# A gated attention unit with a low-rank mixer: the start of the first batch rearranged

## The chip, the cores and the metric

The kernel runs on one core of a Trainium2 chip. The metric is the device time of one execution in microseconds (us). The engines are named as in the profile: PE (TensorE, matrix multiplication), DVE (VectorE), ACT (ScalarE), POOL (GpSimd) and SP (SyncE). POOL and SP here mostly issue transfers; each works through its own queue in order.

## The reference

There are 8 batches, a sequence of S = 3136, a width of 256, and 64 columns in z. Everything comes in and goes out as float32.

```python
scores = (1/S) * z @ z.T                 # per batch, 3136 x 3136, symmetric
attn   = max(scores, 0) ** 2
x      = u * (attn @ v)                  # 3136 x 256
h      = (x.T @ U @ V).T                 # U: 3136 x 32, V: 32 x 3136
y      = x + h
out    = y + max(y @ w_ch1, 0) @ w_ch2   # w_ch1: 256 x 1024, w_ch2: 1024 x 256
```

## The kernel before

**Tiles.** The sequence is cut into 25 tiles: 24 full ones of 128 rows and a last one of 64, whose rows are held twice. All products are in bfloat16. `zT` holds z transposed, with its 64 columns in both halves of the 128 partitions, so that two score matmuls run in the two halves of PE at a time (`score`, L272). ACT applies the ReLU with the scale 1/S (L291) and DVE squares in place (L293). Since the scores are symmetric, only 13 of 25 blocks of each row are computed: `A[j]` is the panel of tile j, with the blocks at distances 0 to 12. The others come by a DMA transpose of a panel into a `strip` (`turn`, L313), issued by SP.

**Attention.** An output tile o is a sum over 25 blocks (`half`, L351), in two halves of PE, into two PSUM banks; two output tiles make a pair. `close_pair` (L365 to L375) adds the two banks (an ACT copy, a DVE add) and multiplies by u on DVE. There are two sets of banks, so a pair can be opened only when the one two before it has been added. Scores are written to PSUM by way of `pair_psum`, which has two buffers.

**Main loop.** For each batch, output tiles are taken in the order 12, 13, ..., 24, 0, ..., 11, while scores of this and the next batch, and the mixer of the batch before, are mixed in between. All five engines' instructions stand in the order in which the program issues them: there is no scheduler, so each engine's order is the order of the calls.

**The start (`start_up`, L607).** In batch 0 no scores exist yet, so the first eight output tiles are made in another way.

1. POOL loads z in three parts, tiles 8 to 16, 0 to 8, 16 to 24, with a cast to bfloat16 (L174), and v in six (L225). DVE copies z twice side by side (`double_z`, L188), PE transposes it against a unit matrix (`turn_on_pe`, L204), and ACT or DVE casts the result into zT (L212).
2. *Side blocks.* For the output tiles 12 to 15, `make(pair)` computes the scores of two tiles j against the four tiles, and `use(pair)`, two pairs later, adds them to the four accumulators. Those of tiles 3 to 11 belong into their panels; the others have room in `v_both[1]` (v of batch 1, not loaded yet) and `x_bf` (L639 to L641). Steps of the list `nxt` stand between: the full score panels of tiles 16 to 19, each with its strip. Then both pairs are closed, one after the other (L686).
3. *Stored blocks.* For the output tiles 16 to 19, `use_stored` takes blocks that lie in panels, `make_stored` computes more of them two pairs ahead, and the remaining twelve blocks of each come from strips (`tail`).
4. Between 2 and 3, w2 is loaded, and z of batch 1 is doubled and transposed as a whole (L695, L696).

The loads of v of batch 1 are issued from the main loop of batch 0 (`v_at`, L781), one part at a time.

Of the kernel before, what the change touches and what calls it, by code (L numbers as in the profile page):

```python
# [42 lines left out]
def kernel(  # L43
# [11 lines left out]
    nc = tc.nc  # L55
# [113 lines left out]
    def load_z(b, parts):  # L169
        if b not in z_raw:  # L170
            z_raw[b] = stage.tile([P, NT, dqk], BF16, name="z_c")
        z_c = z_raw[b]
        for t0, t1 in parts:
            pool_dma(out=z_c[:, t0:t1, :], in_=rows(z[b])[:, t0:t1, :])  # L174
            if t1 == NF:
                for r in halves:
                    pool_dma(out=z_c[r, NF, :], in_=z[b, NF * P :, :])
# [14 lines left out]
    def turn_z(b, parts):  # L192
        z_bf = z_tiles[b]
        for t0, t1 in parts:
            transpose(
                out=zT_of(b)[:, t0 : upto(t1), :],
                in_=z_bf[:, t0 : upto(t1), :, :].rearrange("p t h c -> p (t h c)"),
            )
    def turn_on_pe(parts, banks):

        z_bf = z_tiles[0]
        for (t0, t1), ps in zip(parts, banks):
            for t in range(t0, t1):
                mm(  # L204
                    out=ps[:, (t - t0) * P : (t - t0 + 1) * P],
                    lhsT=z_bf[:, t, :, :].rearrange("p h c -> p (h c)"),
                    rhs=eye,
                    start=True,
                    stop=True,
                )  # L210
            copy = nc.vector.tensor_copy if t0 % 8 else nc.scalar.copy
            copy(  # L212
                out=zT_first[:, t0:t1, :].rearrange("p t c -> p (t c)"),
                in_=ps[:, : (t1 - t0) * P],
            )
# [390 lines left out]

    def start_up():  # L607
        parts = ((8, 16), (0, 8), (16, NF))
        load_z(0, parts[:2])
        nc.gpsimd.memset(eye, 1.0)  # L610
        nc.gpsimd.affine_select(
            out=eye,
            in_=eye,
            pattern=[[1, P]],
            base=0,
            channel_multiplier=-1,
            compare_op=ALU.is_equal,
            fill=0.0,
        )
        load_v(0, (8, 12))  # L620
        load_v(0, (12, 18))
        load_z(0, parts[2:])
        for part in [(3, 8), (0, 3), (18, NF), (NF, NT)]:
            load_v(0, part)
        double_z(0, parts[:2])
        turn_on_pe([(8, 12), (12, 16)], sets[0])
        turn_on_pe([(0, 4), (4, 8)], sets[1])
        nc.gpsimd.memset(U_bf[:, NF, :], 0.0)
        outs = [FIRST + i for i in range(NG)]
        c0 = FIRST * P  # L630
        for o in outs[::2]:
            open_pair(0, o)
            load_u(0, o)
        if B > 1:
            load_z(1, WHOLE)
        for s in fetches[:3]:
            s()
        nxt = [s for j in range(LEAD, LEAD + NG) for s in turned(0, j)]
        rooms = [v_both[1][:, t : t + 4, :] for t in range(0, NF, 4)]  # L639
        rooms = [r.rearrange("p (a t) d -> p a (t d)", a=2) for r in rooms]  # L640
        rooms += [x_bf[:, g].rearrange("p (a w) -> p a w", a=2) for g in (2, 3)]  # L641
        pairs = [(8, 9), (10, 11), (12, 13), (14, 15), (6, 7), (3, 4), (5,), (1, 2)]
        pairs += [(0, 16), (17, 18), (19, 20), (21, 22), (23, 24)]
        where = {}

        def make(pair):
            if all(LEAD - 1 - HALF <= j < FIRST for j in pair):
                todo = []
                for j in pair:
                    at = (FIRST - j) * P  # L650
                    where[j] = A[j][:, at : at + NG * P]
                    todo.append((j, c0, NG * P, where[j]))
                score(0, todo)
            else:
                room = rooms.pop(0)
                for i, j in enumerate(pair):
                    where[j] = room[:, i, :]
                score(0, [(j, c0, NG * P, room) for j in pair])

        seen = []  # L660

        def use(pair):
            for j in pair:
                for o in outs:
                    at = (o - FIRST) * P
                    stop = [o % 2 == 1 and len(seen) == NT - 1 - h for h in range(2)]
                    beside(o, j, where[j][:, at : at + P], stop)
                seen.append(j)

        for i, pair in enumerate(pairs):  # L670
            if i == 3:
                double_z(0, parts[2:])
            if i == 5:
                ps = pair_psum()
                turn_on_pe([(16, 20), (20, NF)], [ps[:, 0, :], ps[:, 1, :]])
                turn_on_pe([(NF, NT)], [pair_psum()[:, 0, :]])
                extend_z(0)
            make(pair)
            if i > 5 and i % 2:
                nxt.pop(0)()  # L680
            if i > 1:
                use(pairs[i - 2])
        for pair in pairs[-2:]:
            nxt.pop(0)()
            use(pair)
        for o in outs[1::2]:  # L686
            close_pair(0, o)

        outs = [LEAD + i for i in range(NG)]
        for o in outs[::2]:  # L690
            open_pair(0, o)
            load_u(0, o)
        fetches[3]()
        if B > 1:
            double_z(1, WHOLE)  # L695
            turn_z(1, WHOLE)  # L696
        pairs = [(j, j - 1) for j in range(LEAD - 1, LEAD - FIRST, -2)]

        def use_stored(js):
            for j in js:  # L700
                for o in outs:
                    if 0 <= o - j <= HALF:
                        beside(o, j, block(0, o, j))

        def make_stored(pair):
            todo = []
            for j in pair:
                k0, k1 = LEAD - j, min(NB, LEAD + NG - j)
                todo.append((j, LEAD * P, (k1 - k0) * P, A[j][:, k0 * P : k1 * P]))
            score(0, todo)  # L710

        nxt += [lambda pair=pair: make_stored(pair) for pair in pairs[:2]]
        own = [lambda j=j: use_stored([j]) for j in outs]
        for s in _merge(nxt, own):
            s()
        rest = []
        for j in range(FIRST - NG, LEAD):
            rest += score_steps(0, j, LEAD + NG - j, NB)
        more = [s for j in range(LEAD + NG, LEAD + 2 * NG) for s in score_steps(0, j)]
        for i, pair in enumerate(pairs):  # L720
            if i + 2 < len(pairs):
                make_stored(pairs[i + 2])
            else:
                more.pop(0)()
            use_stored(pair)
            if i == len(pairs) - 1:
                turn(0, LEAD + NG)
        tail = []
        for o in outs:
            js = [(o + 1 + i) % NT for i in range(HALF)]  # L730

            def close(o=o, j=js[-1]):
                beside(o, j, block(0, o, j), [o % 2 == 1] * 2)
                if o % 2:
                    close_pair(0, o)
                if o == outs[1]:
                    load_u(0, LEAD + NG)
                if o < outs[-1]:
                    turn(0, o + NG + 1)

            for i in range(3):
                some = js[4 * i : min(4 * i + 4, HALF - 1)]
                tail.append(lambda o=o, js=some: [beside(o, j, block(0, o, j)) for j in js])
            tail.append(close)
        for s in _merge(tail, more + rest):
            s()
# [20 lines left out]
    def run(steps):  # L767
        for s in steps:
            s()
# [5 lines left out]
    for b in range(B):  # L775
# [2 lines left out]
        bursts = bursts_of(b - 1) if b else []  # L778
        burst_at = {4: (0, 1), 8: (2, 3), 13: (4, 5), 17: (6, 7)}
        own = own_at if b else first_at  # L780
        v_at = dict(zip((9, 11, 12, 14, 16, 18, 20, 22, 23), V_PARTS)) if b == 0 else {}  # L781
        ahead = dict(zip((2, 3, 6, 7, 10, 11, 14), range(NC)))
        for i in range(begin, NT):
            o = turns(i)
            fill = [s for key in own.get(i, ()) for s in score_steps(b, *key)]
            if more:
                fill += [s for key in next_at[i] for s in score_steps(b + 1, *key)]
                if b and i == 1:
                    load_z(b + 1, WHOLE)
                if b and i == 7:  # L790
                    turn_z(b + 1, ((FIRST, NF),))
                if b and i == 10:
                    turn_z(b + 1, ((0, FIRST),))
                if i == 11:
                    extend_z(b + 1)
                if i in v_at:
                    load_v(b + 1, v_at[i])
            main = attend_steps(b, o)
            if b and i in ahead:
                main.insert(17 if (i + (i > FIRST)) % 2 == 0 else 10, lambda c=ahead[i]: low_rank(b - 1, c))  # L800
# [74 lines left out]
```

## Time and profile before

| | |
|---|---|
| median of 4 runs | 1022.61 us |
| lowest and highest run | 1014.69, 1031.09 us |
| profiled execution | 1012.96 us |
| its span | 1011.3 us |
| PE busy | 986.9 us, 98% of the span |
| ACT busy | 613.3 us, 61% |
| DVE busy | 541.1 us, 54% |
| POOL busy | 171.8 us, 17% |
| moved by DMA | 167.70 MB, mean 166 GB/s |

The profile is that of one execution; its times are counted from the start of its span. A busy share is the time in which an instruction was in work, so a busy engine need not be at its peak. In a line of the order of time the columns are start, duration, engine, line of the program, operation, output and inputs, count, and in brackets the idle time before it with what ended it. Several equal instructions in a row are put together, with their joint duration. A line of a group ends instead with the busy time, the mean of one in nanoseconds, and idle time with what ended most of it. "SPq" is a DMA that SP's queue issued.

### The profile page before, as it was taken

To read this page: it belongs to the slowest core of one execution; us is meant where nothing else is said; L and a number is where in the kernel's file an instruction comes from. 1 tells how busy PE (TensorE), PEld (TensorE's weight loads), DVE (VectorE), ACT (ScalarE), POOL (GpSimd) and SP (SyncE) were. 2 spreads that over 40 slices of the span, in tenths; PEclk is the share of its full clock that TensorE was granted. 3 is DMA by queue.
4 is the path that set the end of the run, shared out by engine and by line. 5 is a ranking of instruction groups with operands and counts; after the bars stand their busy time and mean duration, and the time that the engine had idled before them with its cause. 6 is when DMAs were issued, how large, how long until landed. Compare 5 with 4: busy or idle time off the path is not lost.

```text
span 1011.3 us, 31291 instructions
## 1 busy us (share of the span) xinstructions
PE 986.9 (98%) x13816; PEld 784.8 (78%) x13856; DVE 541.1 (54%) x977; ACT 613.3 (61%) x834; POOL 171.8 (17%) x318
## 2 busy tenths in 40 slices
PE   7799999999999999999999999999999999999998
PEld 5588877787778877788787887878877788777856
DVE  5877654456544664446644556445664356542242
ACT  7886764666645776456764667556674666643154
POOL 4122112121121211121112211112112120011000
PEclk9999999999999999999999999999999999999999
DMA  9999989999998998989989998989989997777532
GB/s 171 153 204 216 185 151 186 179 174 146 165 206 162 176 169 170 166 181 169 160 177 167 182 167 148 191 172 188 151 159 194 168 187 140 143 143 167 105 97 97
DMA packets 414584, 167.70 MB, mean 166 GB/s; under 512 B 389408, under 2 KB 399328, under 8 KB 414448
## 3 DMA queue, kind: packets, MB, share of 16 engines
q1 hardware_dynamic: 384944, 99.16, 61.1%
q0 software_dynamic: 29504, 66.55, 28.5%
q8 instruction: 108, 1.77, 0.7%
q14 instruction: 28, 0.23, 0.1%
HBM read 61.88 MB, written 25.69 MB: 87 GB/s over the span
## 4 chain that ended last, share of the span: by engine, by line
PE 89%; DVE 4%; DMA 3%; ACT 2%; issue 1%; POOL 0%; DVEq 0%; ACTq 0%; POOLq 0%
PE ps L351 46%; PE ps L562 17%; PE ps L520 16%; PE ps L278 6%; ACT A L291 2%; DMA strip<-A 1%; PE ps L385 1%; DVE A L293 1%; PE ps L442 1%; DVE x_bf L502 1%; PE ps L488 1%; DMA out_dram<-o_sb 1%; DVE both L366 1%; DMA zT<-z_bf 1%; DVE x_bf L375 0%
## 5 line engine op out<-in xcount | busy, mean ns | idle before, releaser
L291 ACT ACTIVATE A<-ps 128x832 bf16<-128x832 f32 (+8 forms) x469 | 352.3, 763 | 155.1 <-PE ps L278 141.6
L351 PE MATMUL ps<-v,A 64*128 64x256 bf16 x4864 | 333.1, 269 | 5.8 <-DVE A L293 2.8
L293 DVE TENSOR_TENSOR A<-A 128x832 bf16<-128x832 bf16 (+8 forms) x469 | 240.4, 524 | 146.1 <-ACT A L291 142.1
L351 PE MATMUL ps<-v,strip 64*128 64x256 bf16 x4420 | 306.9, 269 | 0.7 <-DMA strip<-A 0.7
L351 PEld LDWEIGHTS <-A 64*128 64x128 bf16 x4864 | 239.2, 94 | 48.4 <-issue 14.2
L538 ACT ACTIVATE relu_bf<-ps 128x1024 bf16<-128x1024 f32 (+2 forms) x208 | 187.9, 909 | 141.9 <-PE ps L520 139.9
L351 PEld LDWEIGHTS <-strip 64*128 64x128 bf16 x4420 | 222.1, 94 | 34.0 <-DMA strip<-A 0.9
L562 PE MATMUL ps<-w_bf,relu_bf 128*128 128x256 bf16 x1600 | 204.8, 273 | 0.2 <-ACT relu_bf L536 0.2
L573 DVE TENSOR_TENSOR o_sb<-ps,x_bf 128x512 f32<-128x512 f32 (+1 forms) x104 | 69.7, 670 | 248.8 <-PE ps L562 233.7
L520 PE MATMUL ps<-ut,w_bf 128*128 128x512 bf16 (+2 forms) x856 | 197.3, 351 | 2.4 <-ACT relu_bf L538 0.3
L562 PEld LDWEIGHTS <-relu_bf 128*128 128x128 bf16 x1600 | 155.9, 98 | 47.3 <-issue 3.2
L335 POOL DMA_DIRECT2D u_sb<-in_u_dram x96 | 53.4, 556 | 469.3 <-DVE x_bf L375 436.4
L520 PEld LDWEIGHTS <-w_bf 128*128 128x128 bf16 x896 | 85.0, 98 | 61.1 <-issue 7.0
L278 PE MATMUL ps<-zT 64*128 64x416 bf16 (+8 forms) x812 | 131.0, 312 | 0.7 <-ACT A L291 0.7
L365 ACT COPY both<-ps 128x512 f32<-128x512 f32 (+1 forms) x104 | 58.8, 567 | 74.2 <-PE ps L351 66.5
L581 POOL DMA_DIRECT2D out_dram<-o_sb x84 | 46.0, 548 | 272.6 <-DVE o_sb L573 268.6
L366 DVE TENSOR_TENSOR both<-ps,both 128x512 f32<-128x512 f32 (+1 forms) x104 | 69.3, 666 | 27.1 <-ACT both L365 26.7
L375 DVE TENSOR_TENSOR x_bf<-both,u_sb 128x512 bf16<-128x512 f32 (+1 forms) x104 | 69.8, 671 | 3.6
L502 DVE TENSOR_TENSOR x_bf<-ps,x_bf 128x512 bf16<-128x512 f32 (+1 forms) x112 | 65.5, 626 | 8.6 <-PE ps L488 8.6
L278 PEld LDWEIGHTS <-zT 64*128 64x128 bf16 x812 | 42.6, 94 | 4.7 <-issue 0.9
L225 POOL DMA_DIRECT2D v<-in_v_dram x61 | 34.3, 564 | 0.2 <-PE ps L520 0.2
L278 PE MATMUL ps<-relu_bf 64*128 64x416 bf16 (+9 forms) x121 | 22.0, 339 | 2.4 <-ACT A L291 1.3
(52 smaller groups left out, 229.9 us busy)
## 6 DMA issues: line engine op xcount, KB each, us to landing
u_sb<-in_u_dram POOLq DMA_DIRECT2D x96, 256.0 KB, 3.9
out_dram<-o_sb POOLq DMA_DIRECT2D x84, 256.0 KB, 3.2
v<-in_v_dram POOLq DMA_DIRECT2D x57, 192.0 KB, 4.4
strip<-A SPq DMA_TRANSPOSE x196, 5.4
out_dram<-o_sb SPq DMA_DIRECT2D x12, 256.0 KB, 2.1
z_c<-in_z_dram POOLq DMA_DIRECT2D x7, 384.0 KB, 6.1
w_bf<-in_moe_w_ch_dram POOLq DMA_DIRECT2D x2, 512.0 KB, 7.5
u_sb<-in_u_dram POOLq DMA_DIRECT2D x16, 64.0 KB, 2.5
```

What stands on the lines that cost most here:

```text
L278: mm(out=ps[:, k, :n], lhsT=zT[halves[k], j, :], rhs=zT_flat[halves[k], c : c + n], start=True, stop=True,)
L291: nc.scalar.activation(out=dst, in_=src, func=AF.Relu, scale=sc)
L293: nc.vector.tensor_tensor(out=dst, in0=dst, in1=dst, op=ALU.mult)
L351: mm(out=acc[t0][h][:, (o - t0) * D : (o - t0 + 1) * D], lhsT=w[halves[h]], rhs=v_both[b % 2][halves[h], j, :], start=start, stop=stop, **kw,)
L365: nc.scalar.copy(out=both[:, :w], in_=banks[1][:, :w])
L366: nc.vector.tensor_tensor(out=both[:, :w], in0=banks[0][:, :w], in1=both[:, :w], op=ALU.add)
L375: nc.vector.tensor_tensor(out=x_at(b, t0, n), in0=split(both[:, :w]), in1=u_sb[:, :n, :].rearrange("p t (a c) -> p t a c", c=P), op=ALU.mult,)
L502: nc.vector.tensor_tensor(out=q, in0=split(ps[h][:, : len(ks) * D]), in1=q, op=ALU.add)
L520: mm(out=ps[i][:, :w] if apart else ps[:, i, :w], lhsT=w1_bf[:, db, (hp + i) * P : (hp + i + 1) * P], rhs=uT[c][:, db, len(chunks[c]) * P ...
L538: nc.scalar.activation(out=relus[c][:, hp : hp + 2, :w], in_=ps[:, :, :w], func=AF.Relu)
L562: mm(out=ps[:, k * D : (k + 1) * D], lhsT=relus[c][:, ht, q : q + P], rhs=w2_bf[:, ht, :], start=(ht == 0), stop=(ht == NH - 1),)
L573: nc.vector.tensor_tensor(out=o_sb[:p, :nk, :].rearrange("p t (a c) -> p t a c", c=P), in0=split(ps[:p, : nk * D]), in1=x_at(b, t, nk)[:p] ...
```

## The change

All of it lies in `start_up` and its helpers, and in one line of the main loop.

- Tiles 0 to 16 of z of batch 0 are no longer loaded by POOL with a cast, but by SP as float32 into the two buffers for u, and DVE and ACT each make one of the two copies (`first_z`). Ahead of that DVE zeroes 512 columns of a buffer, and PE runs seven matmuls of 512 columns on them whose result is not used.
- Tiles 16 to 24 of z are transposed into one pair of banks and cast by one DVE instruction, not in two groups by ACT and DVE.
- All weights, w2 among them, and then all of v of batch 1, are issued by POOL right after z of batch 1. The loads in the main loop are gone.
- The side blocks that lay in `v_both[1]` and `x_bf` lie in the panels of tiles 20 to 24 and 0 to 2, not yet in use then.
- The last two pairs of side blocks are used first for the output tiles 12 and 13, which are closed, and then for 14 and 15. The stored blocks of step 3 are likewise taken first for 16 and 17. Two steps of `nxt` go ahead of them.
- z of batch 1 is doubled and transposed in two parts, after the second and the third pair of stored blocks.

```diff
+    def first_z(parts):
+
+        z_bf = z_tiles[0] = stage.tile([P, NT, 2, dqk], BF16, name="z_bf")
+        wide = zT_rest[:, :4, :].rearrange("p t c -> p (t c)")
+        nc.vector.memset(wide, 0.0)
+        ps = pair_psum()
+        for _ in range(7):
+            mm(out=ps[:, 0, :], lhsT=zT_rest[:, 0, :], rhs=wide, start=True, stop=True)
+        landed = []
+        for t0, t1 in parts:
+            z_f = u_pool.tile([P, 2, D], FP32, name="u_sb").rearrange("p a c -> p (a c)")
+            z_f = z_f.rearrange("p (t c) -> p t c", c=dqk)
+            nc.sync.dma_start(out=z_f, in_=rows(z[0])[:, t0:t1, :])
+            landed.append(z_f)
+        for (t0, t1), z_f in zip(parts, landed):
+            nc.vector.tensor_copy(out=z_bf[:, t0:t1, 0, :], in_=z_f)
+            nc.scalar.copy(out=z_bf[:, t0:t1, 1, :], in_=z_f)
+
...
-            copy = nc.vector.tensor_copy if t0 % 8 else nc.scalar.copy
+            copy = nc.vector.tensor_copy if t0 % 8 or t1 == NF else nc.scalar.copy
...
-        load_z(0, parts[:2])
+        first_z(parts[:2])
...
-        double_z(0, parts[:2])
         turn_on_pe([(8, 12), (12, 16)], sets[0])
         turn_on_pe([(0, 4), (4, 8)], sets[1])
...
-        for s in fetches[:3]:
-            s()
+        run(fetches)
+        if B > 1:
+            for part in V_PARTS:
+                load_v(1, part)
         nxt = [s for j in range(LEAD, LEAD + NG) for s in turned(0, j)]
-        rooms = [v_both[1][:, t : t + 4, :] for t in range(0, NF, 4)]
-        rooms = [r.rearrange("p (a t) d -> p a (t d)", a=2) for r in rooms]
-        rooms += [x_bf[:, g].rearrange("p (a w) -> p a w", a=2) for g in (2, 3)]
+        rooms = [A[j % NT][:, : 2 * NG * P] for j in range(LEAD + NG, LEAD + 3 * NG)]
+        rooms = [r.rearrange("p (a w) -> p a w", a=2) for r in rooms]
...
             if i == 5:
-                ps = pair_psum()
-                turn_on_pe([(16, 20), (20, NF)], [ps[:, 0, :], ps[:, 1, :]])
+                turn_on_pe([(16, NF)], [pair_psum().rearrange("p a w -> p (a w)")])
...
-        for pair in pairs[-2:]:
+
+        for o in outs[1::2]:
             nxt.pop(0)()
-            use(pair)
-        for o in outs[1::2]:
+            for pair in pairs[-2:]:
+                use(pair, (o - 1, o))
             close_pair(0, o)
...
-        fetches[3]()
-        if B > 1:
-            double_z(1, WHOLE)
-            turn_z(1, WHOLE)
...
-        own = [lambda j=j: use_stored([j]) for j in outs]
-        for s in _merge(nxt, own):
-            s()
+        run(nxt[:2])
+        own = [
+            lambda j=j, some=some: use_stored([j], some)
+            for some in (outs[:2], outs[2:])
+            for j in outs
+            if j <= some[-1]
+        ]
+        run(_merge(nxt[2:], own))
...
-            use_stored(pair)
+            use_stored(pair, outs)
+            if B > 1 and i in (1, 2):
+                part = ((0, FIRST), (FIRST, NF))[i - 1]
+                double_z(1, (part,))
+                turn_z(1, (part,))
...
-        v_at = dict(zip((9, 11, 12, 14, 16, 18, 20, 22, 23), V_PARTS)) if b == 0 else {}
...
-                if i in v_at:
-                    load_v(b + 1, v_at[i])
```

More of the change, by code (lines that the diff above doesn't have):

```diff
@@ L658, in make, with use @@
                 score(0, [(j, c0, NG * P, room) for j in pair])
-        seen = []
-        def use(pair):
+        def use(pair, some):
             for j in pair:
-                for o in outs:
+                for o in some:
                     at = (o - FIRST) * P
-                    stop = [o % 2 == 1 and len(seen) == NT - 1 - h for h in range(2)]
+                    stop = [o % 2 == 1 and j == NF - h for h in range(2)]
                     beside(o, j, where[j][:, at : at + P], stop)
-                seen.append(j)
         for i, pair in enumerate(pairs):
@@ L681, in start_up @@
             if i > 1:
-                use(pairs[i - 2])
-        for pair in pairs[-2:]:
+                use(pairs[i - 2], outs)
+        for o in outs[1::2]:
             nxt.pop(0)()
-            use(pair)
-        for o in outs[1::2]:
+            for pair in pairs[-2:]:
+                use(pair, (o - 1, o))
             close_pair(0, o)
@@ L692, in start_up, with use_stored @@
             load_u(0, o)
-        fetches[3]()
-        if B > 1:
-            double_z(1, WHOLE)
-            turn_z(1, WHOLE)
         pairs = [(j, j - 1) for j in range(LEAD - 1, LEAD - FIRST, -2)]
-        def use_stored(js):
+        def use_stored(js, some):
             for j in js:
-                for o in outs:
+                for o in some:
                     if 0 <= o - j <= HALF:
```

## The prediction

> **What bounds the kernel now.** The engine table of the page comes first: TensorE (PE) is busy for 986.9 us of a span of 1011.3, so all its idle time together is 24.4 us. The table of stretches then shows where that lies (columns: stretch, length, busy time of PE, PE weight loads, DVE, ACT, POOL, clock, DMA share, GB/s).
>
> ```profile
> 0.00:5.00 5.00, 0.00 (x0) 0.00 (x0) 0.56 (x2) 1.28 (x1) 3.83 (x12) 1.00 0.45 55
> 5.00:10.00 5.00, 4.20 (x42) 3.04 (x44) 3.54 (x8) 3.65 (x7) 2.90 (x6) 1.00 1.02 170
> 10.00:15.00 5.00, 3.92 (x60) 2.94 (x58) 3.89 (x9) 3.69 (x7) 3.36 (x7) 1.00 1.12 216
> 15.00:20.00 5.00, 4.40 (x67) 3.50 (x64) 3.11 (x6) 4.50 (x7) 2.30 (x4) 1.00 1.11 241
> 20.00:26.00 6.00, 5.94 (x99) 4.97 (x94) 4.58 (x8) 5.82 (x8) 0.00 (x0) 1.00 0.83 155
> 26.00:34.00 8.00, 4.07 (x50) 2.40 (x47) 7.46 (x14) 5.67 (x10) 2.03 (x3) 1.00 0.63 127
> 34.00:39.00 5.00, 5.00 (x91) 4.48 (x89) 3.65 (x11) 4.57 (x11) 0.00 (x0) 1.00 1.29 144
> 39.00:45.00 6.00, 4.90 (x69) 3.41 (x65) 4.48 (x9) 5.92 (x9) 0.00 (x0) 1.00 1.32 201
> ```
>
> The reader is to see three holes: 5.0 us before the first matmul, 3.9 us of 8 in 26 to 34, where DVE is full (7.46 of 8), and 1.1 us in 39 to 45, where ACT is full. From 60 us on PE has no hole but 0.71 us in 80 to 90, and batches 1 to 6 lose 0.4 to 1.4 us each (120.67 busy of 122, 122.58 of 123). So the change works on the first 60 us, with 13.8 us of idle PE, 5 of them before data. The order of time names what ends each hole:
>
> ```profile
> 5.05 1.89 PE L204 MATMUL ps<-eye,z_bf 128*128 128x128 bf16 x16 [5.05 <-DVE z_bf L188]
> ...
> 29.70 1.87 DVE L188 COPY z_bf<-z_c 128x1600 bf16<-128x1600 bf16 x2
> ...
> 31.60 8.22 SPq L195 DMA_TRANSPOSE zT<-z_bf  x1
> ...
> 32.63 0.28 PE L351 MATMUL ps<-v,A 64*128 64x256 bf16 x2 [1.60 <-DVE A L293]
> ...
> 44.73 0.61 PE L351 MATMUL ps<-v,strip 64*128 64x256 bf16 x8 [0.71 <-DMA strip<-A]
> ```
>
> The first hole waits for z; the second for DVE, which doubles batch 1's z between the closing of two pairs and the next score blocks; the third for a strip transpose queued behind the 8.22 us transpose of batch 1's z.
>
> **Opening.** Before, POOL issues z at 1.30, the chain gives it 3.11 us to 4.41, the doubling ends at 5.05. After, SP issues z in float32 from about 0.8 (its queue waits 0.7 at the start). The nearest row, SP's output stores of 256 KB, has 2.1 us to landing: first part 2.9, second about 4.1 (256 KB more at some 200 GB/s). An ACT copy of 512 float32 takes 0.59 (row of L212), and DVE works beside it: ready at 3.5 and 4.7. The Trainium skill ("Trainium Kernel Development and Optimization", Key Constraints) speaks against a gain here: queues of different engines share the same DMA engines, so another issuer saves only issue time. By that the first part would need POOL's 3.1 us and be ready at 4.5, by the row at 3.5. It hardly matters, since the fill of seven 512-column matmuls takes seven times about 0.43 us (two pairs of such scores took 1.04 us with one latency), 1.1 to 4.1. So PE turns z at 4.1 to 4.5 instead of 5.05.
>
> What the fill itself is worth: the clock column reads 1.00 everywhere, but the same score matmul is longer at first (windows 4.9 to 8.55 and 8.6 to 12.2):
>
> ```profile
> L278 PE MATMUL ps<-relu_bf 64*128 64x512 bf16 x4 | 1.0, 618 | 0.0
> ```
> ```profile
> L278 PE MATMUL ps<-relu_bf 64*128 64x512 bf16 x6 | 1.2, 377 | 0.7 <-ACT A L291 0.7
> ```
>
> The Trainium skill ("TensorE: Matmul & The Clock Gate", Part 1) says that PE runs at half rate until it has been busy for a window of about 3.4 us, free-running, so that its end moves by half a microsecond. By the granted clock the fill gains nothing; by the rule, with which the 618 against 377 ns agree, it takes 0.24 us off the first score and 0.05 us off each transpose. I take the rule. Then: block 8 to 12 turned by 4.6, cast by ACT after its second z copy, 4.7 to 5.3; DVE's cast to 5.6; first score 5.65 instead of 6.87; first ReLU about 6.1 instead of 7.52: 1.4 us. The next release must hold too: v tiles 8 to 12 landed at 7.87 (a POOL wait) for a use at 8.87, tiles 12 to 18 at 10.27 for 11.29. Two z issues of POOL (1.22 us) leave its queue ahead of them, so they should land about 1 us earlier, against uses 1.4 earlier: it holds by about 0.6. I book **-1.3**, between -0.6 (z or v late) and -2.0.
>
> **Turning z tiles 16 to 24 in one piece.** It removes a PE wait of 0.67 between two groups of transposes, and an ACT cast of 0.59; the DVE cast doubles, from 0.69 to at most 1.4. DVE is free for it at 13.2, so it ends near 14.5, where a score took the bank at 14.13 before. **+0.2**, from 0 to +0.4. The eight rooms in panels hold what the v and x buffers held, by the same 1.05 us ReLU and 0.69 us square: no row separates them, 0. No ReLU or square is added or removed.
>
> **Closing interleaved, doubling moved.** From 26.5 DVE has: one square 0.59, four pair operations of 0.685, three squares of 0.59, two of 0.43, together 6.0 us, and 1.87 of doubling. Without it the squares that PE waits for end at 32.5 instead of 33.4. The interleaving lets scores 1.1 us of ACT earlier through, but DVE stays the bound, so only the 0.9 counts. The doubling returns after the second and third stored pair: there PE needs 16 times 0.055 plus 0.21, 1.1 us a pair, 6.5 for six; DVE 4.3 for the squares plus 1.87, 6.2. It fits with 0.3 to spare, and queued behind each copy are the squares two pairs ahead. **-0.8**, from 0 (all given back) to -1.9.
>
> **Order of SP's queue.** Strips 18 and 19 now go ahead of batch 1's transpose, so the 0.71 us stall at 44.73 goes. Next late is strip 20: both z halves (8.22 together) go from about 35.5 to 44, then the strip takes 2.4 (ten in 24.29 us) to 5.4; it is used at 51.75 less the shift, about 49. It fits by 0 to 3 us. **-0.7**, from 0 to -1.1.
>
> **Loads brought forward.** On POOL w2 moves from 30.62 to 18 (0.92 us), and ten issues of v of batch 1 (9 parts, 0.55 us each, 5.4 us in all) from 53 to 97 to behind it. They queue ahead of u for the pairs 16 and 18, issued at 28.75 and 30.09. POOL waits for earlier landings, so bytes set its pace: weights and v, 3.0 MB at about 200 GB/s, 15.4 to 31. u issued at up to 31 lands 4.7 later, and DVE wants it at 45.82: 10 us of cover, cost 0; without cover each microsecond is lost one for one. Strips 16 and 17 share the DMA engines with this burst, and are used at 38.74, 11 us after their time: 0. Later, 1.6 MB of some 9 MB leave 53 to 97, where ACT waits 4.9 us for strips but PE loses only the 0.71: **-0.4**, from 0 to -0.7.
>
> **Sum.** -1.3 +0.2 -0.8 -0.7 -0.4 = -3.0 us. The profiled execution took 1012.96 us (1.66 around the span): 1009.96 after. The four runs have a median of 1022.61, 9.65 above it, and scatter from 1014.69 to 1031.09. I carry the difference over: **1019.6 us**.
>
> **Rivals.** *The opening's holes close as a whole.* Idle PE from 5 to 60 us is 8.8, with 1.3 before and 0.7 in 80 to 90: 10.8, giving 1011.8. For it: every hole named has its cause touched. Against: ACT at 5.82 of 6 and 5.92 of 6, and DVE at 7.46 of 8, fill them with work that is only moved. A variant with the same time: the 9.65 us by which ordinary runs exceed the profiled one are late transfers, and early loads remove most of it; no row shows those runs. Together 0.25.
>
> *SP's queue falls behind, slower.* Place: the line from strip 16 (21.75) to strip 20 (needed at 49), with four strips and z ahead. At the strip median of 2.35 us it holds five strips and z, 20 us of 27; PE waits from a mean of 3.8. With the burst beside it, at 5.4 a strip and z doubled to 16.4, it holds 43.4, 16 late, less 2.3 gained elsewhere: 1036. It is over 1% slower from a mean strip of about 6.4. Against: strips ran at 2.43 with the DMA share at 1.2 to 1.3, and the burst should be over before z turns. With the scatter of the runs, 0.10.
>
> *The change does not do what it says:* z still lands at about 4.4, v binds at 8.87, DVE gives back the doubling: 1022, 0.05.
>
> **How the numbers follow.** The forecast has 0.60. Its parts end at -5.7 and about +0.4, so 1017 to 1023; the scatter of a median of such runs, about 4 us, makes it 1013 to 1027. One percent, 10 us, is about what a measurement of this kernel tells from no change, and it is also nearly all idle time within the change's reach. Reaching toward the first rival, the range is 1009 to 1026. Faster by over 1% 0.25, within 0.65, slower 0.10.
>
> **What would show it.** Right: first transposes of z near 4.1 to 4.5; first score of 512 below 0.45 us; first ReLU near 6.1; use of the first stored pair near 31; no PE wait for a strip below 50 us; no v load between 45 and 100. Wrong: a first wait for v near 7.5, a PE wait for squares behind the doubling, a wait for strip 20, or main-loop idle that differs from 0.4 to 1.4 us a batch.

## The result, and the profile after

The changed kernel is slower by 0.43%: a median of 1020.78 us against 1016.83 us, a ratio of 1.0043 with a 95% interval of 1.0029 to 1.0058. (Some executions of the kernel before fall in a slower state, which the ratio leaves out, so it is not quite the quotient of the medians, 1.0039.) That is inside the one percent band, but on the other side of zero from the forecast of -0.3%. The forecast of 1019.6 us lies near 1020.78 by luck: it started from a median of four runs, 1022.61, and 63 runs of the same kernel give 1016.83.

The profiled execution took 1019.66 us, with a span of 1018.0, 6.7 longer than before. The stretches show where (core 0 of the changed kernel; columns as in the first table: stretch, length, busy time of PE, PE weight loads, DVE, ACT, POOL, clock, DMA share, GB/s).

```profile
0.00:5.00 5.00, 3.74 (x15) 1.72 (x16) 1.18 (x3) 2.63 (x4) 4.26 (x13) 1.00 0.63 147
...
20.00:26.00 6.00, 5.41 (x78) 4.14 (x76) 4.51 (x7) 5.51 (x9) 3.01 (x6) 1.00 1.28 196
26.00:34.00 8.00, 6.65 (x99) 4.91 (x98) 7.67 (x20) 7.78 (x15) 1.57 (x3) 1.00 1.23 172
34.00:39.00 5.00, 1.61 (x25) 0.98 (x21) 2.37 (x6) 1.73 (x2) 1.12 (x2) 1.00 1.38 59
39.00:45.00 6.00, 3.50 (x31) 2.21 (x31) 2.37 (x4) 3.34 (x4) 0.00 (x0) 0.72 1.57 91
45.00:50.00 5.00, 0.84 (x10) 0.59 (x12) 0.00 (x0) 0.00 (x0) 0.00 (x0) 0.66 1.06 186
```

The hole of 26 to 34 is mostly closed (6.65 busy instead of 4.07). In its place stands a new one from 34 to 50, where PE works 5.95 us of 16 and its clock falls to 0.72 and 0.66. The DMA share is at its highest there, 1.57, while only 59 and 91 GB/s move. The order of time on PE says what it waited for:

```profile
4.21 1.75 PE L223 MATMUL ps<-eye,z_bf 128*128 128x128 bf16 x16
...
6.06 0.61 PE L297 MATMUL ps<-relu_bf 64*128 64x512 bf16 x4
...
29.87 1.05 PE L370 MATMUL ps<-v,A 64*128 64x256 bf16 x16 [0.23 <-DVE A L312]
...
39.10 0.61 PE L370 MATMUL ps<-v,strip 64*128 64x256 bf16 x8 [3.49 <-DMA strip<-A]
...
49.16 1.03 PE L370 MATMUL ps<-v,strip 64*128 64x256 bf16 x8 [6.57 <-DMA strip<-A]
```

Up to 29.87 all is early. Then PE waits 3.49 us for the strip of tile 16 and 6.57 us for that of tile 17, 10.1 us in all; before, it waited for one strip, 0.71 us. The same strips as SP's queue ran them (start, duration from issue of the first to landing of the last):

```profile
19.90 29.61 SPq L332 DMA_TRANSPOSE strip<-A  x4
49.63 3.36 SPq L195 DMA_TRANSPOSE zT<-z_bf  x2
```

Strip 16 was issued at 19.90 and landed at 39.05; strip 17 was issued at 25.75 and landed at 49.11. That is 19.1 and 23.4 us, where the same two took 4.2 and 3.7 us before. The DMA view shows what ran beside them. First the kernel before, from 22 to 30 us (queue: packets, MB, share of 16 engines; then issues with the median us to landing):

```profile
q1 hardware_dynamic: 3136, 0.79, 52.3%
q0 software_dynamic: 31, 0.08, 4.9%
...
strip<-A SPq DMA_TRANSPOSE x2, 3.9
```

The kernel after, from 28 to 32 us:

```profile
q0 software_dynamic: 499, 0.67, 93.5%
q1 hardware_dynamic: 491, 0.13, 24.8%
...
strip<-A SPq DMA_TRANSPOSE x1, 23.4
```

Queue 1 carries the transposes, in packets of about 256 bytes (0.79 MB in 3136), and queue 0 carries POOL's loads, in packets of about 1.3 KB. Before, the strips had the DMA engines to themselves. After, the two queues pass packet for packet, 491 to 499, so the loads move five bytes for one of the strips. At 491 packets in 4 us the two strips' 3136 packets take 25.5 us; they took 29.2, from 19.90 to 49.11. That is close, but the rate was not steady: 370 packets in 24 to 28 us, 965 in 32 to 36. The Trainium skill ("DMA: Bandwidth & Descriptors", Queues, rings and completion order) says that each DMA engine takes turns between its queues a packet at a time; the even count of this window agrees, though no run shows that the page's packets are those that the view counts. From 20 to 24 us it does not show: there 1125 packets of queue 0 passed and none of queue 1, although strip 16 had been issued.

How the 6.7 us come together, landmark by landmark (before, after):

| landmark | before | after | shift |
|---|---|---|---|
| first transposes of z | 5.05 | 4.21 | -0.84 |
| first ReLU | 7.52 | 6.49 | -1.03 |
| first score after the second turning of z | 14.13 | 12.26 | -1.87 |
| first pair closed | 28.45 | 26.14 | -2.31 |
| PE ready for the strips | 38.74 | 35.61 | -3.13 |
| third pair closed | 46.51 | 54.87 | +8.36 |
| span | 1011.3 | 1018.0 | +6.7 |

Between the fifth row and the sixth 11.5 us are lost. PE's idle time between these two landmarks grew from 1.14 to 10.09 us, and the two waits are 10.06 of that. Its busy time grew from 6.63 to 9.17 us, for no more matmuls (98 before, 93 after). So about 9.0 of the 11.5 are waiting and 2.5 are slower matmuls, at half clock after idling: eight of one shape take 0.61 us at 39.10 and 1.03 at 49.16. Afterward 1.7 us come back: 0.63 in 80 to 100 us, where the kernel before had a stall, 0.8 up to 170, the rest scattered.

### The profile page after: what moved, and what is told of

Same layout as the page of the kernel before. It is cut to its first block, busy times and chain, and to the rows that moved or that the text cites. A ratio compares the mean times of both kernels' runs of the same rounds, so it can differ in the third digit from the quotient of the medians.

```text
span 1018.0 us, 31319 instructions
## 1 busy us (share of the span) xinstructions
PE 991.9 (97%) x13823; PEld 786.5 (77%) x13863; DVE 540.5 (53%) x978; ACT 614.2 (60%) x835; POOL 170.5 (17%) x316
## 4 chain that ended last, share of the span: by engine, by line
PE 89%; DMA 4%; DVE 4%; ACT 2%; issue 1%; ACTq 0%
PE ps L370 45%; PE ps L581 17%; PE ps L539 17%; PE ps L297 6%; DMA strip<-A 3%; ACT A L310 2%; PE ps L404 1%; DVE A L312 1%; PE ps L461 1%; DVE x_bf L521 1%; PE ps L507 1%; DMA zT<-z_bf 1%; DVE both L385 1%; DVE x_bf L394 0%; PE ps L207 0%
## 5 line engine op out<-in xcount | busy, mean ns | idle before, releaser
L310 ACT ACTIVATE A<-ps 128x832 bf16<-128x832 f32 (+8 forms) x477 | 359.7, 768 | 163.9 <-PE ps L297 152.8
L370 PE MATMUL ps<-v,A 64*128 64x256 bf16 x4988 | 341.5, 269 | 2.4 <-DVE A L312 2.3
L312 DVE TENSOR_TENSOR A<-A 128x832 bf16<-128x832 bf16 (+8 forms) x477 | 245.3, 527 | 157.0 <-ACT A L310 153.5
L370 PE MATMUL ps<-v,strip 64*128 64x256 bf16 x4420 | 309.5, 271 | 10.1 <-DMA strip<-A 10.1
L370 PEld LDWEIGHTS <-A 64*128 64x128 bf16 x4988 | 245.2, 94 | 46.5 <-issue 11.0
```

The costliest lines, as they stand in the source:

```text
L310: nc.scalar.activation(out=dst, in_=src, func=AF.Relu, scale=sc)
L312: nc.vector.tensor_tensor(out=dst, in0=dst, in1=dst, op=ALU.mult)
L370: mm(out=acc[t0][h][:, (o - t0) * D : (o - t0 + 1) * D], lhsT=w[halves[h]], rhs=v_both[b % 2][halves[h], j, :], start=start, stop=stop, **kw,)
```

## The experiments

Each run lists its ratio to the kernel before, with a 95% interval. The kernel before was run again beside each group of experiments (medians from 1014.42 to 1015.84 us), and the ratio is to those runs. "Third pair closed" is the landmark of the table (before 46.51, after 54.87).

**Which load does it.** Three kernels, each the changed one with some loads put back, and one that is the kernel before with the early loads alone.

e1_v_late puts v of batch 1 back into the main loop; w2 stays early:

```diff
-        if B > 1:
-            for part in V_PARTS:
-                load_v(1, part)
...
+        v_at = dict(zip((9, 11, 12, 14, 16, 18, 20, 22, 23), V_PARTS)) if b == 0 else {}
...
+                if i in v_at:
+                    load_v(b + 1, v_at[i])
```

> The changed kernel with one part undone: v of batch 1 is loaded from the main loop again, part by part; w2 stays early. Theory A (the burst of v and w2 starves SP's strip transposes, PE then waits 3.5 and 6.6 us and loses its clock): of some 2.1 MB the 1.6 of v go, strips 16 and 17 land within about 8 us, no PE wait for a strip before 50 us, clock 1.00 in every stretch; third pair closed near 44 us (46.5 before, 54.9 changed), span about 1008, ratio to before about 0.997. Theory B (the loss comes from the new order on SP and DVE itself: strips 18, 19 and two z transposes, the doubling inside the loop): the waits stay, span 1015 to 1018.

Measured: median 1010.12 us, ratio 0.9954 (0.9928 to 0.998). No PE wait for a strip up to 60 us, third pair closed at 44.94. One edit takes 0.9% off the changed kernel and makes it faster than the one before. SP's queue runs the first four strips in 14.15 us instead of 29.61:

```profile
21.84 14.15 SPq L332 DMA_TRANSPOSE strip<-A  x4
```

Strips 16 and 17 took 9.9 and 9.3 us here, with w2 still early: more than the 4.2 and 3.7 of before, but done before PE wanted them. The step from 9.9 and 9.3 to 19.1 and 23.4 is v's. The single profiled execution took longer than that median, 1016.75 us: it lost its time later, beside the v loads (stretches, then ACT in order of time):

```profile
80.00:90.00 10.00, 7.53 (x103) 6.37 (x100) 5.59 (x11) 4.38 (x7) 1.60 (x3) 0.84 1.26 178
```
```profile
84.84 2.43 ACT L310 ACTIVATE A<-ps 128x896 bf16<-128x896 f32 x3 [4.62 <-DMA strip<-A]
```

Of the 20 runs 12 lie below 1010.4 and 19 between 1006.11 and 1020.47. That fits a stall that comes in some executions and not in others, but only one of them has a trace, so it is not shown.

e2_w2_late puts w2 back behind the second closing and leaves v early:

```diff
-        run(fetches)
+        run(fetches[:3])
...
             load_u(0, o)
+        fetches[3]()
```

> The changed kernel with w2 loaded after the first four output tiles again, v of batch 1 still early. Theory A: the burst shrinks from 2.1 to 1.6 MB in front of strips 16 and 17, and w2 is put behind v and two u loads; strip 16 lands some 3 to 5 us earlier, the two PE waits shrink from 10 to 4 to 7 us, span 1012 to 1015. If w2 alone, whose packets are only 512 bytes, is the culprit: no wait for a strip, span about 1008. Theory B: span 1018 as in the changed kernel.

Measured: 1021.5 us, 1.0059 (1.0041 to 1.0078); strip waits 9.1 us, third pair closed at 54.11. w2's place is not the cause.

e3_both_late has both edits together.

> The changed kernel with both undone: v of batch 1 from the main loop, w2 after the first four output tiles. What stays of the change: the fill and z by SP, the rooms in panels, the cast in one piece, the interleaved closing, z of batch 1 in two parts. Theory A: no PE wait for a strip, third pair closed near 43.5 to 44 us, span 1007.5 to 1008.5, ratio about 0.997. Theory B: span 1015 or more.

Measured: 1012.42 us, 0.9991 (0.9967 to 1.0015); strip waits 1.2 us, third pair closed at 43.65. That is the earliest third pair of all, but its profile loses 3.2 us of PE in 70 to 90, again beside the v loads. So the hole at 34 goes with v, as in e1.

e4_burst_alone is the kernel before, with the side blocks in the panels (else v could not be early) and the early loads, and nothing else:

```diff
-        for s in fetches[:3]:
-            s()
+        run(fetches)
+        if B > 1:
+            for part in V_PARTS:
+                load_v(1, part)
...
-        fetches[3]()
...
-        v_at = dict(zip((9, 11, 12, 14, 16, 18, 20, 22, 23), V_PARTS)) if b == 0 else {}
...
-                if i in v_at:
-                    load_v(b + 1, v_at[i])
```

> The kernel before with only the loads brought forward: w2 and v of batch 1 right after the other weights, the side blocks in panels so that v has its place; z, fill, closing and the order of SP's queue as before. Theory A: the loss comes alone, strips 16 and 17 land after 39 us, and the whole z transpose stands between them and strips 18 and 19; third pair closed at 55 to 60 us, span 1018 to 1024, ratio 1.006 to 1.012. Theory B: no loss, span 1011, ratio 1.000.

Measured: 1020.06 us, 1.0055 (1.0035 to 1.0076); third pair closed at 56.77. Its waits of PE (total, times, longest), then its stretches:

```profile
PE ps L351 <- DMA strip<-A: 11.4, 3, 7.1
```
```profile
45.00:50.00 5.00, 0.00 (x0) 0.00 (x0) 0.62 (x2) 0.17 (x1) 0.00 (x0) 0.54 1.43 160
50.00:60.00 10.00, 6.24 (x57) 4.35 (x59) 2.95 (x7) 3.25 (x6) 0.54 (x1) 0.50 1.09 207
```

The loads alone bring the loss into the old kernel, whose opening, closing and queue order are untouched; the panels are not to blame, since e1 has them too and no such loss. The profiled execution took 1026.40 us, near the slowest of the 20 runs, so its waits may be larger than those of a usual one. Here PE idles through 45 to 50 and runs at half clock for the next 10 us: part of the price is the clock.

**Is it the place of the loads, or their sum?** One theory was that the loads hurt only because they stand ahead of strips 16 and 17. Then behind the u loads of the pairs 16 and 18 they would be harmless. e5_v_behind_u does that to the changed kernel:

```diff
-        if B > 1:
-            for part in V_PARTS:
-                load_v(1, part)
...
             load_u(0, o)
+            for part in (V_PARTS[:4] if o == LEAD else V_PARTS[4:]) if B > 1 else ():
+                load_v(1, part)
```

> The changed kernel with one thing moved: the ten loads of v of batch 1 stand behind the u loads of the pairs 16 and 18 (four and six), which wait for the closed pairs at about 26 and 28 us, and so behind strips 16 and 17; w2 stays early. Theory A (what counts is that the burst is ahead of the strips): strips 16 and 17 land by about 30 us, the waits of 3.5 and 6.6 us go; strips 18 and 19 share with v until some 38 us and are wanted at 42 to 44; third pair closed at 44 to 46 us; no v load in the main loop, so none of the stall in 70 to 90 us that the kernels with v there show; span 1006 to 1010, ratio about 0.993. Rival (1.6 MB at once starve the strips wherever they stand): the wait moves to strip 18 and is 5 us or more, span 1013 or more.

Measured: 1024.41 us (4 runs), 1.0095 (1.0058 to 1.0132). The theory fell. The order of time shows that the wait has moved on by one pair:

```profile
40.30 0.61 PE L370 MATMUL ps<-v,strip 64*128 64x256 bf16 x8 [1.80 <-DMA strip<-A]
...
53.59 1.03 PE L370 MATMUL ps<-v,strip 64*128 64x256 bf16 x8 [11.23 <-DMA strip<-A]
```

The third pair is closed at 44.84, as in e1, but the fourth only at 63.24. Here it is strip 18 that is under way beside the 1.6 MB of v: it took 23.8 us.

e8_v_in_three spreads the same loads over three places (three parts each behind the u loads of the pairs 16, 18 and 20):

```diff
+            for part in (V_PARTS[:3] if o == LEAD else V_PARTS[3:6]) if B > 1 else ():
+                load_v(1, part)
...
+                    for part in V_PARTS[6:] if B > 1 else ():
+                        load_v(1, part)
```

> As the run with v behind u, but v in three pieces: three parts behind each of the u loads of 16 and 18, four behind that of 20, which waits for the closing at about 44 us. Theory A: still nothing ahead of strips 16 to 19, a smaller burst beside 18 and 19, but 0.6 MB now beside strips 21 to 23 at 44 to 50 us. If 1.6 MB at once was too much for strips 18 and 19: faster than the run with v behind u by 1 to 3 us. Otherwise equal or slower by up to 2 us, with a PE wait for a strip or an ACT wait in 50 to 60 us.

Measured: 1023.88 us (4 runs), 1.0105 (1.0043 to 1.0166); strip waits 7.2 us. Smaller waits in the trace (7.2 instead of 13.0), no gain that shows in the time; but the profiled execution was the fastest of the four (1017.04), so the trace may not be that of a usual run. At each of the places tried within 20 to 50 us, a strip is hit.

e9_v_by_tile leaves them where the change put them, but loads one tile at a time, so that their packets are smaller (0.33 MB in 729 in the view below):

```diff
-            for part in V_PARTS:
+            for part in [(t, t + 1) for t in range(NF)] + [(NF, NT)]:
```

> The changed kernel with the same early place of v of batch 1, but one tile to a load (64 KB, packets of 512 bytes) where it was three (192 KB, packets of 1536): POOL has at most eight loads under way, so at most 0.5 MB stand beside a strip where it was 1.5. Theory A' (a strip alternates on each DMA engine with the packets of the loads under way, so it takes as long as what is queued beside it, up to 23 us): strips 16 and 17 in 8 to 12 us, landing at 30 and 36; the two waits of 10 us shrink to 0 to 4; POOL's 26 issues of 0.54 us end near 36, u of the pair 16 lands near 41, in time; span 1006 to 1012. Rival (it is the bytes that have to pass before, 2.1 MB, however cut): waits of 8 to 12 us, span 1017 to 1020.

Measured: 1027.56 us, 1.0109 (1.008 to 1.0138), the longest median of all. For the strips it helped (DMA view, 28 to 34 us):

```profile
q1 hardware_dynamic: 1621, 0.41, 90.7%
q0 software_dynamic: 729, 0.33, 57.9%
...
v<-in_v_dram POOLq DMA_DIRECT2D x6, 64.0 KB, 7.7
strip<-A SPq DMA_TRANSPOSE x2, 12.8
```

Strips 16 and 17 took 13.1 and 13.9 us instead of 19.1 and 23.4 (the 12.8 is the median of 17 and 18), and PE waited only 3.0 us for them. About two packets of the strips now pass for one of the loads. Whether that comes from the smaller packets or from POOL having fewer bytes under way, as it waits for landings between small loads, this run does not separate. And POOL's 26 issues are paced by landings and the last came at 47.9, with u of the pair 16 behind them (order of time):

```profile
48.58 0.58 POOL L354 DMA_DIRECT2D u_sb<-in_u_dram  x1 [0.18 <-issue]
...
59.00 0.69 DVE L394 TENSOR_TENSOR x_bf<-both,u_sb 128x512 bf16<-128x512 f32 x1 [15.43 <-DMA u_sb<-in_u_dram]
```

DVE waited 15.43 us for u. So the cover of 10 us that the prediction gave u can be used up.

**What the opening is worth.** Four kernels undo one of its parts each. e6_no_fill is e5 without the memset and the seven matmuls; e7_z_by_pool is e5 with z loaded by POOL and doubled by DVE as before, so that `first_z` holds only the fill.

```diff
-        wide = zT_rest[:, :4, :].rearrange("p t c -> p (t c)")
-        nc.vector.memset(wide, 0.0)
-        ps = pair_psum()
-        for _ in range(7):
-            mm(out=ps[:, 0, :], lhsT=zT_rest[:, 0, :], rhs=wide, start=True, stop=True)
```

> As the run with v behind u, without the zeroing and the seven matmuls of the fill. If the fill is worth what the forecast gave it (0.24 us on the first score, 0.05 on a transpose): first score at 618 ns, first ReLU later by 0.2 to 0.5 us, or less, since z is there at 4.2 us and the fill ends at 4.4; span longer by under 1 us. If a cold start lasts longer without it (clock below 1 in 5 to 15 us): longer by 1 to 3 us.

```diff
         first_z(parts[:2])
+        load_z(0, parts[:2])
...
+        double_z(0, parts[:2])
```

> As the run with v behind u, with tiles 0 to 16 of z loaded by POOL with a cast and doubled by DVE as before; the fill stays. If z by SP is what brings the opening forward: first ReLU 1.0 us later than with z by SP, less what the warm clock takes off (0.3), and the v tiles of batch 0 later by 1.2 us; span longer by about 1 us. If the fill is all of it: no difference.

Measured: e6 1016.83 us, 1.002 (0.9999 to 1.0042), strip waits 4.6; e7 1018.68 us, 1.0037 (0.9998 to 1.0075), strip waits 4.0. Neither is slower than e5: e6 is faster by more than the intervals, e7 within them. With the opening later, the strips meet the loads at another point and wait 4 to 5 us instead of 13. These two therefore say nothing of the opening by itself, except that time won there can be lost to the strips.

On e1, which has no such collision, the same two edits are e10_v_late_no_fill and e11_v_late_z_by_pool.

> The kernel with v of batch 1 from the main loop, which gave a ratio of 0.995, without the fill. What the fill is worth where no burst stands beside it: the clock is granted at 7.9 to 12.5 us as in the traces without a fill, instead of 4.3 to 7.2; first pair closed 1.5 to 2 us later than with the fill (26.1 to 27.1 in five of six traces); ratio 0.996 to 0.998. If the fill is worth nothing: equal to 0.995.

> The kernel with v of batch 1 from the main loop, with tiles 0 to 16 of z loaded by POOL and doubled by DVE as before, fill kept. First transposes at 5.05 instead of 4.21, first ReLU 0.6 to 0.9 us later, first pair closed at 27.5; ratio 0.996 to 0.997. If z by SP is worth nothing: equal to 0.995.

Measured: e10 1010.29 us, 0.9936 (0.9915 to 0.9957), runs from 1008.45 to 1015.31; e11 1012.81 us, 0.997 (0.9945 to 0.9995). Both intervals overlap that of e1 (0.9954), so neither the fill nor SP's load of z has a worth that the time shows. e10 has the lowest ratio of the study, though its interval overlaps that of e1; it is faster than both kernels of the case. Its stretches have no hole at 34 (5.00 of 5), and SP's queue runs four strips in less than half the time:

```profile
26.00:34.00 8.00, 6.64 (x88) 4.46 (x86) 7.25 (x16) 7.87 (x14) 1.11 (x2) 1.00 1.25 176
34.00:39.00 5.00, 5.00 (x87) 4.32 (x82) 4.31 (x12) 4.26 (x8) 0.00 (x0) 1.00 1.26 205
39.00:45.00 6.00, 5.60 (x79) 3.93 (x77) 4.99 (x10) 6.00 (x12) 0.00 (x0) 1.00 1.11 210
...
80.00:90.00 10.00, 10.00 (x178) 8.43 (x176) 8.38 (x16) 9.08 (x13) 1.93 (x3) 1.00 1.24 230
```
```profile
21.91 13.44 SPq L327 DMA_TRANSPOSE strip<-A  x4
35.40 4.83 SPq L195 DMA_TRANSPOSE zT<-z_bf  x2
```

The DMA share is as high here as in the changed kernel (1.25 against 1.23 in 26 to 34). That share does not tell who gets the engines.

**What closing and queue order are worth.** e12_old_closing is e10 with the closing of the side blocks, the order of the stored blocks and the doubling and transpose of batch 1's z as before:

```diff
-        for o in outs[1::2]:
+        for pair in pairs[-2:]:
             nxt.pop(0)()
-            for pair in pairs[-2:]:
-                use(pair, (o - 1, o))
+            use(pair, outs)
+        for o in outs[1::2]:
             close_pair(0, o)
...
+        if B > 1:
+            double_z(1, WHOLE)
+            turn_z(1, WHOLE)
...
+        own = [lambda j=j: use_stored([j], outs) for j in outs]
+        run(_merge(nxt, own))
...
-            if B > 1 and i in (1, 2):
-                part = ((0, FIRST), (FIRST, NF))[i - 1]
-                double_z(1, (part,))
-                turn_z(1, (part,))
```

> The kernel with v of batch 1 from the main loop and no fill (ratio 0.9936, third pair closed at 45.0 us, 46.5 before), with the closing put back as it was: both pairs of side blocks for all four output tiles and then two closings in a row, z of batch 1 doubled as a whole between them and the stored blocks and transposed ahead of strips 18 and 19. If the interleaving and the moved doubling are worth the 0.8 us and the order on SP the 0.7 that the forecast gave them: third pair closed at 46.3 to 46.7, ratio 0.995 to 0.997. If they are worth nothing: 45.0 and 0.9936.

Measured: 1016.07 us (14 runs), 1.0015 (0.9987 to 1.0042). The third pair is closed at 46.41, against 45.01 in e10: closing and queue order together are worth 1.40 us there, by one trace of each. The hole in 26 to 34 is back:

```profile
26.00:34.00 8.00, 4.06 (x50) 2.41 (x48) 7.45 (x14) 5.67 (x10) 1.11 (x2) 1.00 1.15 168
...
70.00:80.00 10.00, 7.88 (x137) 7.18 (x134) 6.27 (x11) 5.82 (x10) 1.10 (x2) 1.00 1.26 178
```

Its profile also has the stall of 70 to 90 us (7.88 of 10) that e1 and e3 have and e10 has not. Its span is 4.2 us above e10's, so 2.8 of that come after the third pair. The timed runs lie further apart still: 1.0015 against 0.9936, with separate intervals, some 8 us. Either closing and queue order are worth more than the landmark shows, or the later stall comes more often with the old ones; no run here decides.

## Why the prediction was wrong

**The step that failed is "Loads brought forward"**, in its sentence "Strips 16 and 17 share the DMA engines with this burst, and are used at 38.74, 11 us after their time: 0". Eleven microseconds were the cover, and the strips were late by more: they took 19.1 and 23.4 us instead of 4.2 and 3.7. The term should have read +11.5: about 9.0 of added waiting and 2.5 of matmuls at half clock. e1 shows it by taking v away (1.0043 becomes 0.9954), e4 by bringing the loads alone into the old kernel (1.0055).

Three things went wrong in that step. The durations of the strips came from rows of before in which no load ran beside them: POOL's queue had 31 packets in 22 to 30 us. That "strips ran at 2.43 with the DMA share at 1.2 to 1.3" was taken as proof that they bear a load beside them; but in the profile before, in 34 to 45 us, SP's transposes themselves took 97.6% of the engines' time and POOL's loads 32.0%, so most of that share was the transposes' own. And the burst was taken to be over at 31 us by dividing bytes by 200 GB/s; the last loads of v landed at 45.17 to 46.95 and the u loads at 48.46 and 49.04.

On u the same step was wrong as well, and only luck hid it. It had u issued at up to 31 and landed 4.7 us later. The changed kernel shows the issue (POOL in order of time) and the time to landing (DMA view, 34 to 44 us):

```profile
34.36 0.58 POOL L354 DMA_DIRECT2D u_sb<-in_u_dram  x1 [0.92 <-DVE A L312]
...
u_sb<-in_u_dram POOLq DMA_DIRECT2D x2, 256.0 KB, 13.8
```

DVE wanted u of the pair 16 at 45.82, less the 3.13 gained by then, so at 42.69; it landed at 48.46. Without the late strips DVE would have waited some 5.8 us for it (an estimate from these figures). With them the pair was closed only at 54.87, and nothing waited for u.

**The rival "SP's queue falls behind"** had the right line of SP's queue and the right mechanism: a burst beside the strips, PE waiting for them. It was priced at 5.4 us a strip, taken from rows without a burst, with its worst case at 1036, and set aside at 0.10 because "the burst should be over before z turns". The strips came to 19 to 23 us each, but only two of them, and z was not doubled: strip 18 took 12.9 us, strip 19 7.2, the halves of z 3.8 and 6.1. Strips 18 and 19 had landed within 2.6 us of strip 17, and PE waited for no later strip up to 60 us. So it was slower, by less than one percent.

**The page on shared engines was put to the wrong step.** The prediction weighed, for the load of z, that queues of different engines share the DMA engines. There the measurement lies between its two forecasts. SP's first part was issued at 0.81 and landed at 3.50, 2.7 us later, where the row had 2.1; POOL's in e11 was issued at 1.30 and landed at 4.39, 3.1 later. So about half of the 0.9 us gained is the earlier issue. The first part was copied at 4.12, where 3.5 was named by the row and 4.5 by the page. The sharing was not weighed for the strips, where it cost the time.

**Opening, -1.3.** Right in the changed kernel's trace: first transposes at 4.21, scores at 377 ns instead of 618 from the first on, first ReLU 1.03 earlier. It is right as a trace, but not proved as time: e10 without the fill has the cold 610 ns again and is not slower than e1. The two traces have first pairs closed at 28.15 and 28.08; in e1's the clock fell back to half from 8.27 to 11.68 us, so it does not show the fill at work.

**Turning z tiles 16 to 24 in one piece, +0.2.** Wrong in sign: the shift grows from -1.03 to -1.87 there. The removed wait of 0.67 counts, and the longer cast does not: it ran on DVE from 12.11 to 13.33 and the score at 12.26 did not wait for it but for ACT's short cast, 0.35 us.

**Closing and doubling, -0.8; order of SP's queue, -0.7.** Together 1.5, and e12 measures 1.40 at the third pair (its timed runs differ by more, as said). The use of the first stored pair came at 29.87, where 31 was named. The two parts were not taken apart.

**Later gain, -0.4.** In the changed kernel the main loop gets back more, 1.7 us. But the kernels with v in the main loop are faster in all, so this gain was not worth its price.

**The base.** The 9.65 us carried from the profiled execution to the median were 3.9 by 63 runs (1016.83 against 1012.96). So the base was 5.8 too high, and the sum 7.0 too low (-3.0 against 1020.78 less 1016.83, which is +4.0); the two errors nearly cancel in the number.

**Left open.** Why no packet of queue 1 passed from 20 to 24 us. Why the strips' packets were still slow once most of the burst had gone (DMA view of the changed kernel, 34 to 44 us):

```profile
q1 hardware_dynamic: 1592, 0.40, 103.4%
q0 software_dynamic: 313, 0.35, 50.4%
```

Five packets of queue 1 now pass for one of queue 0, so taking turns packet by packet no longer explains it; each holds its engine for 104 ns (16 engines by 10 us by 1.034, by 1592), where the 5818 transpose packets of before in 34 to 45 us held it for 30. Nothing here tells what they waited for. Then, what makes the stall of 70 to 90 us come in the traces of e1, e3, e11 and e12 but not in that of e10. Last, why e10 gains 6.5 us by its ratio (0.64% of 1015.84) but only 3.2 by its span: the medians of the kernel before exceed its profiled execution by 1.5 to 3.9 us, that of e10 by half a microsecond, and no trace shows those runs.

## What to carry to other kernels

A bulk load that is moved to an earlier place is to be priced by what runs beside it there, not by when its own data are wanted; small-packet transfers such as DMA transposes, issued on another queue, can take five to six times as long (19.1 and 23.4 us against 4.2 and 3.7), and the duration read from a trace without such a neighbour is no estimate. Look in the DMA view, in the stretch that receives the load, at which queue has the packets: a busy share near full says nothing of who is served. And when a cover is compared with a delay, estimate the delay as packets times the turn they get (here 25.5 us, where 29.2 were measured at an unsteady rate), before calling it zero. A cover that was not used up is no proof either: see whether something else was later still, as the strips were later than u.

## What the runs showed of the hardware

- Beside the loads of v, strips of 0.39 MB took 19.1 and 23.4 us; with these loads gone 9.9 and 9.3 (e1), and with w2 gone from there too 7.4 and 4.2 (e3); in the kernel before they took 4.2 and 3.7. In 28 to 32 us one packet of the strip passed for one of the loads (491 to 499). With the loads cut to one tile each the two took 13.1 and 13.9 (e9).
- PE that waits also loses its clock. In e4 the granted clock was at half for 17 us, from 45.41 to 62.48, around two waits for strips of 7.13 and 2.57 us, and the changed kernel had it at half for 10.2 us in two pieces, in steps of 3.41 us. The Trainium skill ("TensorE: Matmul & The Clock Gate", Part 1) names a window of this length. So an idle stretch of PE can cost more than its own length: 2.5 us more in the changed kernel.
- The first record of the full clock came between 4.26 and 7.21 us in the nine kernels that have the fill of PE, at 7.86 and 7.87 in the two that load z by POOL without it (e4 and the kernel before), and at 11.42 to 12.52 in the three that load z by SP without it; but in e1 the clock then fell back to half from 8.27 to 11.68. The clock column reads 1.00 also where no record lies, as in the first 7.87 us of the kernel before, so the prediction's "By the granted clock the fill gains nothing" had no record behind it.
